# 256 units of a mixture layer kept per batch, not 512, with 256 more checked by signs

## The chip, the core and the metric

The kernel runs on one core of a Trainium2 chip. The metric is device time in microseconds of one execution on that core. Engines are named as the profile names them: PE (TensorE; PEld is its weight load), DVE (VectorE), ACT (ScalarE), POOL (GpSimd), SP (SyncE, which here only issues DMAs). A row "y<-vv,hh 128x256" reads: the instruction writes tile y from tiles vv and hh, 128 partitions by 256 elements.

## The reference

Attention through 49 agents feeds a mixture of eight experts, of which each token uses one. B, N, C = 4, 11456, 128; F = 1024 units per expert.

```python
agent_v = softmax(scale * agents @ k.T) @ v     # per batch: 49 x 128
x = softmax(scale * q @ agents.T) @ agent_v     # per token: 49 weights, then 128 values
e = argmax(x @ w_gate)
h = relu(x @ w1[e])                             # 1024 units
out = gate * sigmoid(x @ w_output_gate)[e] * (h @ w2[e])
```

A token enters only through its 49 weights, so `x @ w1[e]` is a product of those weights with the 49 x 1024 table `agent_v @ w1[e]`.

## The kernel before, in words

**Batches and units.** Each of the four batches has 12 units of tokens (eleven of 1024 and one of 192). For k a unit gives agent scores (tiles `ks`, `S`, `mx`), for v a weighted sum (`ev`, `av`), for q the token weights. When all k and v units of a batch are done, `folded` takes the agent averages, `choose` picks the expert that the batch's mean token would use, and its two weight matrices are loaded.

**Kept and linear units.** `hidden` (line 978) makes the 49 x 1024 table and a number g per unit, the smaller the more mixed the signs of its column. The 512 units with the smallest g are kept: `sel` gathers them, `ha` and `hr` make their first-layer weights `w` and `wr`, and `second` makes their second-layer weights `vv`. The others are taken to be of one sign for nearly all tokens, so that their relu is the identity or zero, and `linear` folds them into one matrix `G` (tile `gw`). A bound on g and on the token's squared weights (`thr`, `qe`) tells for which tokens this holds.

**A tile of 512 tokens** (92 tiles: 88 whole, four of 192). Single precision is carried as two half-precision parts. `q_rest` (line 1182) turns a unit's scores into weights `ef` and parts `e`; a transposing DMA puts them into `x_ld` (49 high rows, 49 low rows, 30 high rows again). `mm1` (line 1363) multiplies by `w` into four banks `h` and adds the 19 rows that did not fit by `wr`; for this three further DMAs copy rows of `x_ld` to other row groups (`x2`). `relu` takes `hh` (high part, ACT) and `hl` (rest, DVE) of each bank. `mm2` (line 1396) multiplies `gw`, and then `hh` and `hl` of each of four groups by `vv`, into `y`. `finish` adds the two halves of `y` (ACT `ys`, DVE `os`), `store` scales on POOL and writes out. Per unit `q_rest` also makes the eight expert logits (`lg`), the gate, and a flag per token.

**Left-over tokens.** Flagged tokens, and tokens of another expert, are gathered after the last unit of batches 0 and 1 (phase 0), and of 2 and 3 (phase 1): 14 tiles and 4 tiles of 128, exactly, in single precision (`let`, `lx`, `lh`, `ly`), with the expert's weights loaded anew for each. A loop behind them runs only when more tiles are needed.

**What sets the order.** The program is written by generators that a planner (`Clock`, `tick`) steps by estimated times; the result is one fixed list of instructions for each engine. Each engine runs its list in order. `spawn(g, prio)` gives the generator's rank, `LEFT` that of the left-over tiles, `ITEMS` (line 1338) the order in which k, v and q units are loaded and multiplied. On PE score products are written as blocks of 32 weight columns; when PE's list has a gap, as blocks of 64.

Of the kernel before, what the change touches and what calls it, by code (L numbers as in the profile page):

```python
# [17 lines left out]
P = 128  # L18
# [3 lines left out]
NBM = 4  # L22
NS = NBM * P
NG_ = 64
MARK = 1024.0
# [6 lines left out]
YS = 2  # L32

LARGE, SMALL, KEEP = 7, 8, 3
# [8 lines left out]
G4 = 4  # L43
# [11 lines left out]
K_W = K_GAM + NG_  # L55
# [4 lines left out]
QUIET = 4500.0  # L60
# [215 lines left out]
def agent_attention_top1_moe(ctx, tc, qT, kT, v, aT, wg, wo, w1, w2, cst, sides, slots, out):  # L276
# [53 lines left out]
    def group_free():  # L330

        if not all(banks[k][0] for k in range(G4)):
            return None
        return max(when_free(banks[k]) for k in range(G4))
# [39 lines left out]
    gam = kc[:, K_GAM:K_GAM + NG_]  # L374
    iot = cp.tile([P, NS], F16, name="iot")
# [3 lines left out]
    for i in range(2):  # L379
        t = cp.tile([P, 2, C], F16, name=f"gw_{i}")  # L380
        POOL.memset(t[:, 1, :], 0.0)
        gw.append(t)
    idle_x = cp.tile([P, 256], F16, name="idle_x")
# [10 lines left out]
    for i in range(4):  # L394
        t = cp.tile([P, 8, P], F16, name=f"e16_{i}")
        e16s.append(t)
# [74 lines left out]
    busy = {"w12": False, "sel": False}  # L471
# [104 lines left out]
    def scored(item):  # L576
        places[held.pop(item)][0] = True

# [112 lines left out]
    def v_weights(b, u, M):  # L691
# [8 lines left out]
        else:  # L700
            e = wk.tile([P, 4, C], F32, name=f"ev{b}_{u}", tag="os", bufs=4).rearrange("p t c -> p (t c)")
# [45 lines left out]
    def v_turned(u):  # L747
# [3 lines left out]
        if u in (0, FIRST):  # L751
            while not any(banks[k][0] for k in range(G4, 8)):
                yield None
            k = min((when_free(banks[k]), k) for k in range(G4, 8) if banks[k][0])[1]
# [10 lines left out]
        if u == NU - 4:  # L765
            others[:] = range(G4, 8)
# [18 lines left out]
    def shares():  # L785
# [9 lines left out]
        rec = wk.tile([P, A2], F32, name="rec0", tag="rec0")  # L795
# [104 lines left out]
    def choose(b, x, ad):  # L900
# [26 lines left out]
        while busy["w12"]:  # L927
            yield None
# [21 lines left out]
    def gates(b, ad):  # L950

        ab = wk.tile([P, A], F32, name=f"ab{b}", tag="ab")
# [25 lines left out]
    def hidden(b, ad, w1t, w2t):  # L978
# [34 lines left out]
        gv, gs = tl("hgv", C, F32, "avn")[:, 0:NG_], tl("hgs", 1)  # L1013
        yield from DVE.q.scalar_tensor_tensor(gv, c[:, 0:NG_], NS + 0.5, gam, op0=ALU.is_le, op1=ALU.mult)
        release(mark)
        yield from DVE.q.tensor_reduce(gs, gv, axis=AX.X, op=ALU.max)
        m, inc = tl("hm", NB), tl("hinc", NB)
# [6 lines left out]
        yield from DVE.q.scalar_tensor_tensor(inc, m, MARK, inc, op0=ALU.mult, op1=ALU.add)  # L1024
        yield from DVE.q.tensor_tensor(inc, c[:, 0:1].broadcast_to([P, NB]), inc, op=ALU.add)
# [3 lines left out]
        sel = wk.tile([P, NB, NS], F16, name=f"sel{b}", tag="sel16", bufs=1)  # L1029
        for n in range(NB):  # L1030
            yield from DVE.q.tensor_scalar(sel[:, n, :], iot, inc[:, n:n + 1], None, op0=ALU.is_equal)
# [955 lines left out]
```

## Time and profile before

| | |
|---|---|
| median of 3 runs (range) | 865.51 us (864.14 to 873.72) |
| profiled execution | 866.38 us, span 864.6 us |
| mean granted PE clock | 0.956 |
| busy PE, DVE, ACT, POOL | 735.0, 640.3, 445.8, 410.5 us |
| main tiles run | from 74.8 us to about 767 us |
| share of the 16 DMA engines by the main queue | 60.2% |

Busy time of PE counts each matmul from its issue to its modelled end, and matmuls overlap; how many fit into a stretch is read from the distance of their starts. Busy time of DVE, ACT and POOL is the time in which at least one instruction runs. An engine's idle time matters only where another waits for it.

### The profile page before, as it was taken

The page shows a single profiled execution, that of the slowest core. Times are in us where ns is not written, and L with a number is a line of the kernel's source. Part 1 is how long each engine was busy: PE and PEld are TensorE (multiplying, and loading weights), DVE is VectorE, ACT ScalarE, POOL GpSimd, SP SyncE. Part 2 cuts the span into 40 slices and gives each one's busy share as a digit, 9 for nine tenths or more (in the row PEclk, how much of TensorE's full clock was granted, in tenths as well). Part 3 has the DMA queues.
Part 4 walks back from the last instruction along what each step waited for, and adds up shares of the span by engine and source line. Part 5 has one row for each costly group of instructions (what it writes and reads, how often), then busy time and mean ns, then how long its engine had stood idle before and what let it go on. Part 6 is the DMA issues. An engine that isn't in the chain of part 4 may idle for free. (4 is left out here: it accounts for less than half of the span.)

```text
span 864.6 us, 31825 instructions
## 1 busy us (share of the span) xinstructions
PE 735.0 (85%) x12969; PEld 581.2 (67%) x12969; DVE 640.3 (74%) x2029; ACT 445.8 (52%) x1129; POOL 410.5 (47%) x794
## 2 busy tenths in 40 slices
PE   9989977889878998898998988877899999948644
PEld 8777755666666676666776666665687777847634
DVE  2945858878887888999897899878887999542210
ACT  2433645656645665657565655563575675413112
POOL 1001515766442587743443777543567465533131
PEclk9999989999999999999999999999999999969668
DMA  9993674866866777783587886754555343545312
GB/s 330 346 267 88 180 191 139 207 197 192 233 172 150 226 189 194 194 252 110 128 230 230 204 213 176 188 153 115 170 153 150 107 140 128 164 134 169 141 24 103
DMA packets 110039, 152.93 MB, mean 177 GB/s; under 512 B 62878, under 2 KB 71230, under 8 KB 109888
## 3 DMA queue, kind: packets, MB, share of 16 engines
q1 hardware_dynamic: 108160, 148.79, 60.2%
q0 software_dynamic: 1728, 2.06, 1.0%
q8 instruction: 103, 1.69, 0.8%
q14 instruction: 48, 0.39, 0.2%
HBM read 95.27 MB, written 35.43 MB: 151 GB/s over the span
## 5 line engine op out<-in xcount | busy, mean ns | idle before, releaser
L226 PE MATMUL y<-vv,hh 128*128 128x256 f16 (+1 forms) x1440 | 283.7, 274 | 0.1
L226 PE MATMUL y<-vv,hl 128*128 128x128 f16 (+1 forms) x1440 | 261.6, 219 | 1.2 <-issue 1.2
L226 DVE SCALAR_TENSOR_TENSOR hl<-h,hh 128x512 f16<-128x512 f32 (+1 forms) x368 | 226.0, 667 | 41.3 <-ACT hh L226 40.8
L226 ACT ACTIVATE hh<-h 128x512 f16<-128x512 f32 (+1 forms) x368 | 186.8, 591 | 74.9 <-PE h L226 74.5
L226 PEld LDWEIGHTS <-hh 128*128 128x128 f16 (+1 forms) x1440 | 142.2, 99 | 20.4 <-issue 2.2
L226 PEld LDWEIGHTS <-hl 128*128 128x128 f16 (+1 forms) x1440 | 143.4, 100 | 5.0 <-issue 1.7
L226 PE MATMUL y<-gw,x_ld 128*128 128x256 f16 x360 | 76.2, 275 | 52.6 <-DVE os L226 31.5
L226 ACT COPY ys<-y 128x256 f32<-128x256 f32 x179 | 67.0, 376 | 96.5 <-PE y L226 88.7
L226 POOL TENSOR_TENSOR os<-os,smt 128x512 f32<-128x512 f32 (+1 forms) x91 | 95.7, 1052 | 39.3 <-DVE os L226 31.9
L226 PEld LDWEIGHTS <-x_ld 128*128 128x128 f16 (+1 forms) x720 | 55.6, 100 | 75.8 <-issue 62.2
L226 PE MATMUL h<-x_ld,w 128*128 128x512 f16 (+1 forms) x368 | 104.9, 377 | 1.2 <-DVE hl L226 1.2
L226 DVE TENSOR_TENSOR os<-y,ys 128x256 f32<-128x256 f32 x179 | 73.7, 414 | 32.5 <-ACT ys L226 31.6
L226 POOL TENSOR_TENSOR e<-ef,e 128x392 f16<-128x392 f32 (+1 forms) x48 | 42.5, 886 | 33.9 <-ACT e L226 33.7
L226 PE MATMUL ks<-at,k_ld 128*32 128x50 f32 (+1 forms) x2120 | 51.4, 220 | 7.4 <-issue 7.0
L226 PEld LDWEIGHTS ks<-at,k_ld 128*32 128x32 f32 (+1 forms) x2120 | 44.2, 124 | 17.0 <-issue 12.1
L226 POOL TENSOR_TENSOR ev<-S,km_o 128x400 f32<-128x400 f32 (+1 forms) x36 | 33.0, 915 | 39.2 <-PE av L226 35.8
L226 PE MATMUL qs<-at,q_ld 128*32 128x50 f32 (+1 forms) x2768 | 44.8, 213 | 2.3 <-issue 1.3
L226 PEld LDWEIGHTS <-w 128*128 128x128 f16 x368 | 34.1, 101 | 18.1 <-issue 2.4
L226 PEld LDWEIGHTS qs<-at,q_ld 128*32 128x32 f32 (+1 forms) x2768 | 37.6, 113 | 11.6 <-issue 6.4
L226 ACT COPY S<-ks 128x400 f32<-128x400 f32 (+1 forms) x48 | 23.0, 480 | 39.0 <-PE ks L226 38.9
L226 PE MATMUL h<-x_ld,wr 19*128 19x512 f16 (+1 forms) x368 | 37.5, 384 | 3.1 <-DMA x_ld<-x_ld 3.1
L226 ACT ACTIVATE ef<-qz 128x392 f32<-128x392 f32 (+1 forms) x48 | 24.8, 516 | 26.5 <-DVE qz L226 22.6
(316 smaller groups left out, 1440.7 us busy)
## 6 DMA issues: line engine op xcount, KB each, us to landing
v_ld<-v SPq DMA_DIRECT2D x44, 512.0 KB, 4.6
q_ld<-qT SPq DMA_DIRECT2D x44, 512.0 KB, 4.0
out<-os SPq DMA_DIRECT2D x88, 256.0 KB, 4.5
k_ld<-kT SPq DMA_DIRECT2D x43, 512.0 KB, 4.5
lws<-w SPq DMA_DIRECT2D x18, 512.0 KB, 4.4
lw<-w SPq DMA_DIRECT2D x18, 512.0 KB, 4.1
efd<-ef SPq DMA_DIRECT2D x44, 200.0 KB, 4.4
x_ld<-x_ld SPq DMA_DIRECT2D x132, 64.0 KB, 3.5
```

The source lines that it names most:

```text
L226: return getattr(self.eng, op)(*a, **k)
```

## The change

256 units are kept per batch (`NBM` 2), so a tile has two groups, and `wr` is a 128-row tile with zeros below row 32, used without copies of `x_ld`. The next 256 units by g are linear as well, but each token is tested for them: `second_bound` finds them in two steps of 64 thresholds, and makes `wc`, the 49 x 256 table with each column's sign turned to that of its sum and its entries lowered by a small margin; `signs` multiplies each 128 tokens' high parts by `wc` (tile `ck`) and sums relu of the negated products on ACT (`cx`, `vs`). A token with a sum above zero is flagged. Beyond these 512 units the old bound holds. The logits are summed in PSUM, and some small steps of `q_rest` go from POOL to DVE or back. k and v units of all later batches follow the q units at a fixed rate of 2.2, where they came batch by batch; left-over tiles get rank 2, and their weights are loaded ahead into tiles of their own.

```diff
-NBM = 4
+NBM = 2
 NS = NBM * P
+NC_ = 256
+HB = 3
...
+OSN = 4
+FRONT, BACK = 6, 4
+
+LARGE, SMALL, KEEP = 7, 6, 3
...
-QUIET = 4500.0
+QUIET = 0.0
...
+    half_used = set()
+
+    def used(item):
+
+        if item in half_used:
+            scored(item)
+        else:
+            half_used.add(item)
...
-        yield "PE", [ax, sel], [o], 1
-        clk.vt["PE"] += TURN
         for n in range(NB):
-            for k in range(G4):
-                PE.matmul(o[32 * k:32 * k + 32, 0:P], ax[:, n, P:P + 32], sel[:, n, k * P:(k + 1) * P],
-                          start=(n == 0), stop=(n == NB - 1))
-        clk.vt["PE"] += TURN
-        rest = wk.tile([P, P], F16, name=f"wr{b}", tag="w0")
-        yield from DVE.q.tensor_copy(rest, o[:, 0:P])
+            yield from PE.q.matmul(o[0:32, 0:NS], ax[:, n, P:P + 32], sel[:, n, 0:NS], start=(n == 0), stop=(n == NB - 1))
+        rest = wrs[b % 2]
+        yield from DVE.q.tensor_copy(rest[0:32], o[0:32, 0:NS])
...
+        spawn(second_bound(b, g, m, gs, gc, gv, gs2, n1, m2, inc2, s_, tsv, sel), -1)
+        yield from linear(b, w2t, lin, tsv)
+    def second_bound(b, g, m, gs, gc, gv, gs2, n1, m2, inc2, s_, tsv, sel):
...
+        for step in range(2):
+            cmp_ = tl("hcm2", NB * NG_, F16).rearrange("p (n k) -> p n k", k=NG_)
+            yield from DVE.q.tensor_tensor(cmp_, gf.unsqueeze(2).broadcast_to(bc), gam2.unsqueeze(1).broadcast_to(bc),
+                                           op=ALU.is_lt)
...
+            for n in range(NB):
+                yield from PE.q.matmul(c[:, 0:NG_], idle_w, cmp_[:, n, :], start=(n == 0), stop=(n == NB - 1))
+            yield from DVE.q.scalar_tensor_tensor(gv, c[:, 0:NG_], n1, gam2, op0=ALU.is_le, op1=ALU.mult)
+            release(mark)
+            yield from DVE.q.tensor_reduce(dl if step else gs2, gv, axis=AX.X, op=ALU.max)
+            if step == 0:
+                yield from DVE.q.tensor_scalar(gf, g, gs2, float(NG_), op0=ALU.subtract, op1=ALU.mult)
+        yield from DVE.q.scalar_tensor_tensor(m2, gf, dl, m, op0=ALU.is_lt, op1=ALU.subtract)
...
+        for n in range(NB):
+            yield from DVE.q.tensor_scalar(sel[:, n, NS:NS + NC_], iot, inc2[:, n:n + 1], None, op0=ALU.is_equal)
...
+        o = bank(f"hd{b}")
+        mark = hold()
+        for n in range(NB):
+            yield from PE.q.matmul(o[0:A, 0:NC_], ac[:, n * A:(n + 1) * A], sel[:, n, NS:NS + NC_], start=(n == 0),
+                                   stop=(n == NB - 1))
+        wc = wcs[b % 2]
+        yield from ACT.q.copy(wc, o[0:A, 0:NC_])
+        release(mark)
+        st["wc"] = wc
...
-        while me > 3 and rests[me - 4] < 3 or me > 1 and not state.get(0, {}).get("w"):
+        while me >= FRONT and rests[me - FRONT] < 3 or me > 1 and not state.get(0, {}).get("w"):
...
-        while vacant_turned() is None:
-            yield None
-        x2 = place(("x2", b, u), vacant_turned()[1], [1024], F16)
-        for g in range(1, G4):
-            yield from SY.q.dma_start(x2[32 * g:32 * g + 32, 0:nt * pp], x1[0:32, 0:nt * pp])
-        X1[b, u] = x1, x2
+        X1[b, u] = x1
...
-            yield from PE.q.matmul(lg[0:pp, t * 36:(t + 1) * 36], x1[:, t * pp:(t + 1) * pp],
-                                   gs.rearrange("p k c -> p (k c)"), start=True, stop=True)
+            for k in range(2):
+                yield from PE.q.matmul(lg[0:pp, t * 18:t * 18 + 17], x1[:, t * pp:(t + 1) * pp], gs[:, k, 0:17],
+                                       start=(k == 0), stop=(k == 1))
...
+        L = lg[0:pp, 0:nt * 18].rearrange("p (t a) -> p t a", a=18)
+        lm, d, d256, rr = tl("lm"), tl("ld_", E), tl("d256"), tl("rr")
+        yield from DVE.q.tensor_reduce(lm, L[:, :, 0:E], axis=AX.X, op=ALU.max)
+        yield from DVE.q.tensor_tensor(d, L[:, :, 0:E], lm.unsqueeze(2).broadcast_to([pp, nt, E]), op=ALU.subtract)
+        yield from DVE.q.tensor_scalar(d256, L[:, :, 16], 1e-9, None, op0=ALU.add)
+        lo = tl("lo", E)
+        yield from ACT.q.copy(lo, L[:, :, E:2 * E])
+        vs = wk.tile([P, 8], F32, name=f"vs{b}_{u}", tag="vs", bufs=BACK)
+        spawn(signs(b, u, me, x1, vs), 1)
+        yield from POOL.q.tensor_scalar(rr, d256, s3[0:pp], None, op0=ALU.mult)
+        yield from DVE.q.reciprocal(rr, rr)
...
+        while me not in signed or "thr" not in state[b]:
+            yield None
         yield from DVE.q.scalar_tensor_tensor(d256, e2[0:pp, 0:nt], state[b]["thr"][0:pp], d256, op0=ALU.mult, op1=ALU.is_gt)
-        yield from POOL.q.tensor_tensor(og, d256.unsqueeze(2).broadcast_to([pp, nt, E]),
-                                        state[b]["dom"][0:pp].unsqueeze(1).broadcast_to([pp, nt, E]), op=ALU.mult)
-        yield from POOL.q.tensor_tensor(og, og, ndom[0:pp].unsqueeze(1).broadcast_to([pp, nt, E]), op=ALU.add)
+        yield from DVE.q.scalar_tensor_tensor(d256, vs[0:pp, 0:nt], 0.0, d256, op0=ALU.is_gt, op1=ALU.max)
+        yield from DVE.q.tensor_tensor(og, d256.unsqueeze(2).broadcast_to([pp, nt, E]),
+                                       ndom[0:pp].unsqueeze(1).broadcast_to([pp, nt, E]), op=ALU.max)
...
+    def signs(b, u, me, x1, vs):
+
+        base, pp, nt = UNITS[u]
+        while "wc" not in state[b] or me > 0 and me - 1 not in signed:
+            yield None
+        wc = state[b]["wc"]
+        for t in range(0, nt, 2):
+            yield from wait_free()
+            o = bank(f"ck{b}_{u}_{t}")
+            mark = hold()
+            for j in range(2):
+                yield from PE.q.matmul(o[0:pp, j * NC_:(j + 1) * NC_], x1[0:A, (t + j) * pp:(t + j + 1) * pp], wc,
+                                       start=True, stop=True)
+            for j in range(2):
+                x = wk.tile([P, NC_], F16, name=f"cx{b}_{u}_{t + j}", tag="cx", bufs=1)
+                yield from ACT.q.activation(x[0:pp], o[0:pp, j * NC_:(j + 1) * NC_], AF.Relu, scale=-1.0,
+                                            accum_out=vs[0:pp, t + j:t + j + 1])
+            release(mark)
+        used(("x1", b, u))
+        signed.add(me)
...
+        kv = [(kind, b, u) for b in range(1, B) for kind in "kv" for u in range(PRE if (kind, b) == ("k", 1) else 0, NU)]
+        qs = [("q", b, u) for b in range(B) for u in range(NU)][2:]
+        for i, x in enumerate(qs):
+            items.append(x)
+            n = max(0, int(RATE * (i + 1)) - int(RATE * i))
+            items += kv[:n]
+            del kv[:n]
...
+    RATE = 2.2
...
-    OFF = 8
-    RING = 12
+    OFF = 4
+    RING = 10
...
-        x1, x2 = (x[:, 512 * h:512 * h + w] for x in X1[b, u])
-        p = []
-        for g in range(G4):
-            p.append((bank(f"h{i}_{g}", k=g), hold()))
-            PE.matmul(p[g][0][:, 0:w], own_[:, g * P:(g + 1) * P], x1, start=True, stop=False)
-            if g < G4 - 1:
-                tick()
-        for g in range(G4):
-            rows = slice(32 * g, 32 * g + AR)
-            PE.matmul(p[g][0][:, 0:w], rest[rows, :], (x2 if g else x1)[rows, :], start=False, stop=True)
-        for g in range(G4):
-            spawn(relu(i, g, *p[g]), 0)
-        tick(0)
+        x1 = X1[b, u][:, 512 * h:512 * h + w]
+        for g in range(NBM):
+            o, mark = bank(f"h{i}_{g}", k=(NBM * i + g) % HB), hold()
+            PE.matmul(o[:, 0:w], own_[:, g * P:(g + 1) * P], x1, start=True, stop=False)
+            tick()
+            PE.matmul(o[:, 0:w], rest[:, g * P:(g + 1) * P], x1, start=False, stop=True)
+            spawn(relu(i, g, o, mark), 0)
+            tick()
...
-            if m1 < NT and G4 * (m1 + 1) - freed <= RING and group_free() is not None and group_free() <= now + 20.0:
+            if m1 < NT and NBM * (m1 + 1) - freed <= RING and group_free(m1) is not None and group_free(m1) <= now + 20.0:
...
-    LEFT = 5
-
-    ready, averaged = {}, {}
+    LEFT = 2
...
-                while (ph, k) not in ready or i > finished[0] + 1 or planning() or all(busy.values()):
+                while (ph, k) not in known or i > finished[0] + 1 or busy["own"] and (busy["sel"] or planning()):
                     yield None
-                home = "w12" if busy["sel"] else "sel"
+                home = "sel" if busy["own"] else "own"
                 busy[home] = True
-                t, ti, kk, _, ef, _, xt, two = ready[ph, k]
+                w1t, w2t = yield from left_load(ph, *known[ph, k], f"{ph}_{k}", home)
...
-        spawn(left_prepare(ph), 3 - 2 * ph)
+        spawn(left_prepare(ph), 1.5)
```

PE's list at a main tile. Before, in batch 3: the last of four products by `w`, four by `wr`, a block of q scores, then the first product of the second layer.

```order
L226 LDWEIGHTS w_13580
L226 MATMUL h_3_14055<-x_1_ld,w_13580 128x512
L226 LDWEIGHTS wr_13662
L226 MATMUL h_0_14036<-x_1_ld,wr_13662 128x512
L226 LDWEIGHTS wr_13662
L226 MATMUL h_1_14040<-x_1_ld,wr_13662 128x512
L226 LDWEIGHTS wr_13662
L226 MATMUL h_2_14047<-x_1_ld,wr_13662 128x512
L226 LDWEIGHTS wr_13662
L226 MATMUL h_3_14055<-x_1_ld,wr_13662 128x512
L226 MATMUL qs_5_14020<-at,q_5_ld 32x50 x32
```

Now, in batch 0:

```order
L231 LDWEIGHTS w_1302
L231 MATMUL h_0_4351<-x_10_ld,w_1302 128x512
L231 LDWEIGHTS wr_87
L231 MATMUL h_0_4351<-x_10_ld,wr_87 128x512
L231 LDWEIGHTS w_1302
L231 MATMUL h_1_4361<-x_10_ld,w_1302 128x512
L231 LDWEIGHTS wr_87
L231 MATMUL h_1_4361<-x_10_ld,wr_87 128x512
L231 MATMUL avn_4374<-kc,avd_104 49x128
```

Two banks are written instead of four, and each pair of products follows on its own bank. Over the whole list the products with `hh` and with `hl` fall from 1440 to 720 each, and 360 products `ck` of 256 columns are new.

ACT's list around two main tiles before, where the four `hh` stand together:

```order
L226 COPY ys_0_9860<-y_0_9833 128x256
L226 COPY ys_1_9889<-y_1_9857 128x256
L226 ACTIVATE ef_3_9874<-qz_3_9791 128x8x49
L226 ACTIVATE hh_0_9909<-h_0_9887 128x512
L226 ACTIVATE hh_1_9912<-h_1_9893 128x512
L226 ACTIVATE hh_2_9915<-h_2_9895 128x512
L226 ACTIVATE hh_3_9917<-h_3_9903 128x512
L226 ACTIVATE qz_3_9791<-ef_3_9874 128x8x49
```

Now, at the start of batch 2 (the `cx` belong to units of batch 1):

```order
L231 ACTIVATE hh_1_8116<-h_1_8109 128x192
L231 COPY ys_0_8166<-y_0_8118 128x256
L231 COPY lo_11_8174<-lg_11_8040 96x16
L231 ACTIVATE cx_8_2_8170,vs_8_7399<-ck_8_2_8162 128x256
L231 ACTIVATE cx_8_3_8182,vs_8_7399<-ck_8_2_8162 128x256
L231 ACTIVATE ef_0_8178<-qz_0_8134 128x8x49
L231 COPY ys_1_8204<-y_1_8163 128x256
L231 ACTIVATE cx_8_4_8207,vs_8_7399<-ck_8_4_8194 128x256
```

The 360 sums `cx` stand singly or in pairs between the copies `ys` and the steps of `q_rest`; the `hh` fall from 368 to 184.

PE's list behind the last product of the main tiles. Before (the first six of its rows; left-over tiles 8 to 13 of phase 0 and the table and 4 tiles of phase 1 follow):

```order
L226 MATMUL y_0_16931<-vv_13526,hl_3_16776 96x128
L226 MATMUL tbs_12_17004<-big_3_17000,ones 128x16
L226 MATMUL pbs_12_17022<-pptsb_0_9968,big_3_17000 128x128 x2
L226 MATMUL let_8_17032<-kc,big_2_16112 98x128
L226 MATMUL lx_8_17039<-let_sb_8_17034,lav_11411 128x128
L226 MATMUL lh_8_0_17057<-lxs_8_17046,lws_8_17009 128x128 x4
```

Now, where only phase 1 is left (its table, `pexc`, stands before the last tiles):

```order
L231 MATMUL y_0_15183<-vv_10630,hl_1_15061 96x128
L231 MATMUL tbs_0_15245<-big_0_15241,ones 128x32
L231 MATMUL pbs_0_15257<-pptsb_1_15125,big_0_15241 128x128 x4
L231 MATMUL let_0_15341<-kc,big_0_15241 98x128
L231 MATMUL lx_0_15345<-let_sb_0_15343,lav_15239 128x128
L231 MATMUL lh_0_0_15356<-lxs_0_15347,lw_0_15261 128x128 x4
```

Six left-over tiles and the table of phase 1 moved from behind the last main tile to between the main tiles.

## Rows read from the trace of the kernel before

**Rows 1.** Busy time of each engine in three stretches (before the first main tile, main tiles, behind the last): bounds and length in us, PE, PEld, DVE, ACT, POOL busy us (with instructions), granted PE clock, DMA share, GB/s.

```profile
0.00:75.00 75.00, 70.66 (x1058) 57.93 (x1059) 41.37 (x122) 24.93 (x60) 8.24 (x27) 0.98 0.81 274
75.00:767.00 692.00, 607.39 (x11543) 470.63 (x11541) 577.28 (x1800) 399.56 (x1016) 376.28 (x740) 0.98 0.64 175
767.00:865.00 98.00, 57.00 (x369) 52.62 (x369) 21.68 (x107) 21.26 (x53) 25.93 (x29) 0.74 0.35 118
```

**Rows 2.** The same view, shorter stretches.

```profile
350.00:400.00 50.00, 46.15 (x806) 35.61 (x805) 46.74 (x156) 34.76 (x93) 28.16 (x64) 1.00 0.73 200
...
275.00:400.00 125.00, 111.82 (x2362) 85.16 (x2360) 111.50 (x333) 80.28 (x205) 77.28 (x160) 1.00 0.74 202
...
610.00:767.00 157.00, 145.01 (x1826) 117.59 (x1822) 126.83 (x406) 91.47 (x235) 86.55 (x169) 0.99 0.47 139
...
825.00:850.00 25.00, 15.24 (x103) 13.97 (x104) 4.25 (x20) 5.85 (x15) 6.07 (x6) 0.72 0.28 94
```

**Rows 3.** Who waited for whom, on ACT and on DVE: us in total, times, longest.

```profile
ACT ys L226 <- PE y L226: 89.7, 84, 3.6
...
DVE hl L226 <- ACT hh L226: 40.8, 49, 3.2
```

**Rows 4.** PE's timeline in batch 1: start us, us of the merged run, instruction, count.

```profile
299.83 0.27 PE L226 MATMUL y<-gw,x_ld 128*128 128x256 f16 x1
299.94 0.27 PE L226 MATMUL y<-vv,hh 128*128 128x256 f16 x1
300.05 0.22 PE L226 MATMUL y<-vv,hl 128*128 128x128 f16 x1
300.11 0.27 PE L226 MATMUL y<-vv,hh 128*128 128x256 f16 x1
...
301.26 1.03 PE L226 MATMUL h<-x_ld,w 128*128 128x512 f16 x4
302.22 0.40 PE L226 MATMUL h<-x_ld,wr 19*128 19x512 f16 x4
302.55 0.92 PE L226 MATMUL qs<-at,q_ld 128*32 128x50 f32 x64
303.39 0.28 PE L226 MATMUL y<-gw,x_ld 128*128 128x256 f16 x1
...
305.12 0.18 PE L226 MATMUL lg<-gs,x_ld 128*128 128x36 f16 x1
305.15 0.27 PE L226 MATMUL y<-vv,hh 128*128 128x256 f16 x1
```

**Rows 5.** Groups of instructions by shape on ACT and DVE: count, busy us, mean ns of one, idle before.

```profile
L226 ACT ACTIVATE hh<-h 128x512 f16<-128x512 f32 x352 | 182.8, 602 | 70.0 <-PE h L226 69.5
L226 ACT COPY ys<-y 128x256 f32<-128x256 f32 x176 | 65.9, 376 | 94.4 <-PE y L226 87.4 <-DVE os L226 3.6 <-issue 1.3
...
L226 DVE SCALAR_TENSOR_TENSOR hl<-h,hh 128x512 f16<-128x512 f32 x352 | 221.2, 681 | 39.5 <-ACT hh L226 39.0
...
L226 DVE TENSOR_SCALAR rr<-d,s_s 128x8 f32<-128x8 f32 x44 | 13.8, 316 | 0.0
L226 DVE TENSOR_TENSOR oh<-lr,rm 128x64 f32<-128x64 f32 x44 | 13.6, 310 | 0.1
...
L226 DVE SCALAR_TENSOR_TENSOR a<-se,d 128x8 f32<-128x8 f32 x44 | 11.4, 260 | 0.3
L226 DVE TENSOR_SCALAR sel<-iot,hinc 128x512 f16<-128x512 f16 x32 | 9.5, 366 | 0.0
...
L226 DVE TENSOR_TENSOR hcmp<-hg,kc 128x512 f16<-128x512 f32 x4 | 2.8, 693 | 0.0
```

**Rows 6.** ACT's timeline: two activations with a sum, and a copy of 256 columns with what follows it.

```profile
53.15 0.64 ACT L226 ACTIVATE wsq<-w1t 128x512 f16<-128x512 f32 x1
53.68 0.20 ACT L226 ACTIVATION_READ_ACCUMULATOR wsq<-w1t 128x1 f32 x1
53.77 0.63 ACT L226 ACTIVATE wsq<-w1t 128x512 f16<-128x512 f32 x1
...
300.48 0.40 ACT L226 COPY ys<-y 128x256 f32<-128x256 f32 x1
300.73 0.57 ACT L226 ACTIVATE qz<-ef 128x392 f32<-128x392 f32 x1
```

**Rows 7.** Timelines of PE and DVE behind the last main tile: the table of phase 1 (`pexc`, `tbs`), its index, its first tile (`let`), and the products of its second and last tile.

```profile
788.36 0.29 PE L226 MATMUL pexc<-tot,kc 128*128 128x16 f32 x2
...
803.51 0.61 PE L226 MATMUL tbs<-big,ones 128*128 128x32 f32 x2 [6.23 <-DVE big L226]
...
813.53 0.17 DVE L226 CAST lrus<-lrgs 128x4 uint32<-128x4 f32 x1
826.41 0.53 DVE L226 TENSOR_TENSOR big<-big,lppxs 128x360 f32<-128x360 f32 x1 [12.71 <-DMA big<-cumd,lrus]
...
833.18 0.45 PE L226 MATMUL let<-kc,big 128*98 128x128 f32 x1 [14.80 <-DVE big L226]
...
840.98 1.95 PE L226 MATMUL lh<-lxs,lw 128*128 128x128 f32 x16
842.78 2.33 PE L226 MATMUL ly<-lw,lh 128*128 128x128 f32 x16
...
852.38 2.05 PE L226 MATMUL ly<-lw,lh 128*128 128x128 f32 x16
```

More of the change, by code (lines that the diff above doesn't have):

```diff
@@ L382, in agent_attention_top1_moe @@
         gw.append(t)
+    wrs = []
+    for i in range(2):
+        t = cp.tile([P, NS], F16, name=f"wr_{i}")
+        POOL.memset(t, 0.0)
+        wrs.append(t)
+    wcs = [cp.tile([A, NC_], F16, name=f"wc_{i}") for i in range(2)]
     idle_x = cp.tile([P, 256], F16, name="idle_x")
@@ L470, in agent_attention_top1_moe @@
     state = {}
-    busy = {"w12": False, "sel": False}
+    busy = {"own": False, "sel": False}
     picking = [True]
@@ L751, in v_turned @@
         if u in (0, FIRST):
[L752 removed]
+            while not any(banks[k][0] for k in range(HB, 8)):
                 yield None
[L754 removed]
+            k = min((when_free(banks[k]), k) for k in range(HB, 8) if banks[k][0])[1]
             k0["avp"] = bank(f"avT{u}", k=k), hold()
@@ L1038, in hidden @@
         for n in range(NB):
-            yield from PE.q.matmul(o, ax[:, n, 0:P], sel[:, n, :], start=(n == 0), stop=(n == NB - 1))
+            yield from PE.q.matmul(o[:, 0:NS], ax[:, n, 0:P], sel[:, n, 0:NS], start=(n == 0), stop=(n == NB - 1))
         w = wk.tile([P, NS], F16, name=f"w{b}", tag="w1")
-        yield from ACT.q.copy(w, o)
+        yield from ACT.q.copy(w, o[:, 0:NS])
         release(mark)
@@ L1190, in q_rest @@
         yield from DVE.q.tensor_reduce(m[0:pp, 0:nt], sv, axis=AX.X, op=ALU.max)
+        while me > 1 and me - 2 not in squared:
+            yield None
         z = wk.tile([P, 8, A2], F32, name=f"qz{b}_{u}", tag="qz", bufs=2)
@@ L1274, in q_rest @@
         yield from DVE.q.reciprocal(T, a_)
-        while not {"i12", "thr"} <= state[b].keys():
+        while "i12" not in state[b]:
             yield None
@@ L1427, in finish @@
         if k == 0:
-            while i > 3 and i - 4 not in done or i > 1 and i - 2 not in summed:
+            while i >= OSN and i - OSN not in done or i > 1 and i - 2 not in summed:
                 yield None
-            OS[i] = wk.tile([P, 4, C], F32, name=f"os{i}", tag="os", bufs=4)
+            OS[i] = wk.tile([P, 4, C], F32, name=f"os{i}", tag="os", bufs=OSN)
+        while i not in OS or k > halves.get(i, 0):
+            yield None
         os = OS[i]
@@ L1825, in planning @@
     def planning():
-        return any(K[b]["v"] >= NU - 3 and not (state.get(b, {}).get("vv") and "G" in state[b]) for b in K)
+        return any(K[b]["v"] >= NU - 3 and not (state.get(b, {}).get("vv") and {"G", "wc"} <= state[b].keys()) for b in K)
     def left_static():
```

187 lines of the change are left out of this document (103 added, 84 removed).

## The prediction

> **What bounds the kernel now.** The first view is the table of engine busy time by stretch [rows 1]. Nothing of the main tiles runs in the first 75 us, in which the keys and values of batch 0 are loaded and its weights prepared. Then come 692 us of main tiles, and 98 us of left-over tiles. In the main stretch DVE is busy for 577.3 us, 83.4%, PE for 607.4 us by modelled ends, ACT for 399.6, POOL for 376.3; the DMA engines work 64% of it. So two engines share the bound. Shorter stretches show it [rows 2]: DVE reaches 93.5% from 350 to 400 us, and 89.2% from 275 to 400; from 610 to 767, where no key or value work is left, PE is at 92% and DVE at 81%.
>
> The waits [rows 3] say the same from the other side: ACT's largest, 89.7 us, is for `y` of PE, and DVE's largest, 40.8 us, for `hh`, which itself follows PE. ACT has room, and what waits on it waits in turn for PE.
>
> How much PE can be relieved is read from the distance of starts on its timeline [rows 4], not from busy time. A 256-column product takes 0.11 us to the next start, a pair `hh`, `hl` 0.17 (299.94 to 300.11), four products by `w` 0.96 (0.24 each), four by `wr` together 0.33, a block of q scores 0.84, one `lg` 0.03.
>
> **The main tiles on PE.** Half a tile has two `gw` products and eight pairs: 0.22 + 8 x 0.17 = 1.58 us. With two halves, 0.96 + 0.33 for the first layer and four `lg`, a tile costs 3.16 + 1.29 + 0.12 = 4.57. After, there are four pairs per half, 2 x (0.22 + 0.68) = 1.80; two products by `w`, 0.48; two by the full-height `wr`; four `ck` of 256 columns, 0.44; eight narrower `lg`, at most 0.24. For `wr` the rows give two ends, 2 x 0.33 / 4 = 0.17 as now and 2 x 0.24 = 0.48 as for `w`; since it now has all 128 rows and follows `w` on its own bank, I take 0.48. The tile is 3.44 us, 1.13 less, and 88 whole tiles and four of three eighths make 89.5: **101 us off PE**. The Trainium skill, "TensorEngine Tiling (Array Packing)", section "When to Use Tiling", speaks against this edit: a contraction of 32 rows should use fourfold row tiling. The trace agrees, in that four `wr` of 19 rows take 0.33 us; by that rule alone a packed `wr` would save a further 0.31 us per tile, some 28 us of PE.
>
> **DVE.** It loses half the `hl`: 176 x 221.2 / 352 [rows 5] = 111 us. Per unit of `q_rest` it loses two small steps (`rr`, the sum of the logits) and gains four (the logits' difference, `ogs` by `rr`, the maximum with `vs`, the flag's spreading). Net two steps in 48 units, at 0.26 to 0.32 us as `a` and `rr` are: 28 us. `sel` is written in 64 half-width instructions, not 32: its 9.5 us stay or double, I take 5 more. `second_bound` has per batch two comparisons of 512 like `hcmp` (1.4), one of 392 (0.6), 14 small ones at about 0.28 (3.9): 24 us in four batches. Six left-over tiles and a table come in from behind the main tiles, with about half of the 21.7 us that DVE has there [rows 1]: 10 us. Main stretch: 577 - 111 + 28 + 5 + 24 + 10 = **533 us**.
>
> **ACT.** 184 `hh` go, 93 us (0.52 each in the group [rows 5]). 360 `cx` come. The lower end of one is from the timeline [rows 6]: a 256-column copy hands on after 0.25 us, and reading a sum adds 0.09 (53.68 to 53.77): 0.34. The upper end is the whole of both, 0.376 + 0.20 = 0.58. That is 122 to 207 us; in a queue that has other work behind each, the lower end is nearer, and I take 0.40, 144 us. Some 17 us come with the six left-over tiles and the second bound. Sum: 400 - 93 + 144 + 17 = 468 us, 531 at the upper end.
>
> **The rest.** POOL loses three 64- or 128-column steps per unit and gains one small one, and takes no wait with it. The three row copies per unit leave SP's queue and the DMA engines; the transposing DMA is now the last step ahead of `mm1`, but it also was before for the first group, and units are prepared some tiles ahead. The added wait of `q_rest` for `signs` delays the flags and the gathered rows, not `smt`, which `store` needs; up to four units may hang there. The even flow of k and v puts their blocks beside all q units; the last batches' averages are ready sooner (`ha` of batch 3 stands 228 of 360 `gw` products into PE's list, before at 268, its batch starts at 270), so a batch change should cost less; I count nothing for it. DMA work is 64% of the main stretch now and comes to about 72% of a 610 us one, with fewer bytes: covered; where a load is late, `scores` waits first. PE's list has more 64-wide blocks, which the planner writes only into its gaps.
>
> **Front and tail.** Before the first tile `ha` and four `sel` shrink by about 1 us: 74. Behind the last main tile PE's list now has only the index of phase 1 and 4 tiles. From `tbs` at 803.5 [rows 7] to the end of the span that is 61 us, in which DVE waited 12.7 us for gathers (issued behind scatters of phase 0 that will be done by then), 5 of which I take off; for the part of the table that may still be open I add 4. Tail: **60 us**, where it was 98. The six tiles cost PE in the main stretch 6 x (1.80 + 2.05 + 0.6 for `let` and `lx`) = 27 us.
>
> **The sum.** PE by starts: 89.5 tiles of 4.57 are 409 us, some 115 blocks 97, eight left-over tiles 36, and the products per batch about 35 by my estimate: 577. After: 577 - 101 + 27 + 3 = 506. So DVE with 533 is the fullest. In the old main stretch it ran at 83.4%, where it set the pace at 89.2%, at best at 93.5%. PE falls behind it, but ACT comes closer; I take 87%: 533 / 0.87 = 613. Total 74 + 613 + 60 = 747, and 1.8 us lie outside the span in the profiled execution of before (866.38); the median is 0.9 below that. **748 us, 13.6% less.**
>
> **Rivals.**
> 1. *Denser.* With PE relieved and batch changes smoothed, DVE runs at 93.5% throughout: 533 / 0.935 = 570, total 706. For it: DVE's waits [rows 3] go back to PE. Against: ACT. Chance 0.20.
> 2. *ACT's sums delay the relus.* `hh` stands in one queue behind `cx`, so the three `h` banks come free late, and DVE waits more than now. At the upper price ACT has 531 us, as much as DVE, and two full engines in a row run at 80% or worse: 533 / 0.80 to 533 / 0.74, total 804 to 858. Chance from 775 up 0.16.
> 3. *Slower than before: the sums end on the path.* If each `ck` holds a bank and each `cx` is waited for before the next `hh` can go, then the chain PE to ACT to PE sets the pace: 692 - 101 + 27 + 207 = 825, total 961. It decides from the point where the main stretch exceeds 738 us (874 in total), which is 120 of the 207 us, 0.33 us of every `cx`. For it: 4 `cx` per tile stand among 2 `hh` and 2 `ys`. Against: nothing of the next tile needs a `cx`, five banks are left besides the three. Chance 0.09.
> 4. *The clock falls.* Granted was 0.72 of full speed in the tail, with PE at 61% busy, and 1.00 where it was at 89% [rows 2]. With gaps in every tile, at 0.72 throughout, PE has 506 / 0.72 = 703 us and is the bound: total 839. The Trainium skill, "TensorE: Matmul & The Clock Gate", section "HAM oscillation — how this bites in real kernels", describes this: a loop in which PE runs dry in every round starts each round at the lower clock. By starts PE would be 506 / 613 = 83% full, as before (577 / 692 = 83%), so the trace gives it little: 0.04.
> 5. *More left-over tiles.* The new flags could take more than 14 and 4 tiles and start the loop at the end, at some 45 us per tile (index 30, one tile with its loads 15 [rows 7]). Worked out on the reference's inputs, flagged and foreign tokens go from 1346 to 1352 in phase 0 and from 368 to 371 in phase 1, still 14 and 4 tiles. Chance 0.02, total 793.
>
> **Numbers.** The forecast's own case, DVE at 83.4 to 89.2%, spans 733 to 775 and has 0.49. With rival 1 down to 695 (it may also be that DVE's load is 10 us less) and rival 2 up to 815, with rival 5, about 0.8 is held: 695 to 815. About 1% can be told from no change. Faster by more: 0.49 + 0.20 + 0.15 + 0.02 + part of rival 4, 0.87. Within 1%: 0.04. Slower: 0.09.
>
> **What would show it.** In the changed profile: 184 `hh` and `hl`; 360 `cx` with their reads, 0.34 to 0.58 us each; DVE busy near 570 us in all; ACT near 515; PE's `wr` 0.24 apart; only four `let` behind the last `y`, and some 60 us there. It is wrong if ACT's waits on PE stay at 90 us while PE waits for `hh`, if the granted clock drops below 0.9 in the middle, or if DVE falls below 80%.

## The result and the profile after

The changed kernel took **804.3 us** (median of four executions, 795.7 to 809.0), the kernel before 866.8 beside it; their ratio is 0.920 (95% interval 0.909 to 0.930). That ratio rests on the two shorter of the four, so the better reference is the first experiment below, the same kernel again: **807.8 us** (six executions, 806.7 to 811.5), ratio 0.934 (0.930 to 0.938). The kernel is faster, and within the range given; but the gain is 58 to 63 us, where 118 were forecast. The execution profiled is the shortest, 795.7 us with a span of 794.0.

First the busy time by stretch, with the columns of [rows 1]: before the first main tile, main tiles, behind the last.

```profile
0.00:68.00 68.00, 65.01 (x1007) 54.27 (x1008) 41.76 (x121) 24.92 (x62) 9.24 (x30) 0.97 0.86 296
68.00:734.00 666.00, 593.69 (x9169) 435.04 (x9168) 537.46 (x1863) 462.62 (x1592) 361.38 (x668) 0.94 0.63 178
734.00:794.00 60.00, 22.99 (x154) 21.15 (x151) 13.63 (x55) 9.63 (x24) 14.47 (x15) 0.68 0.27 86
```

Read length against length: the front went from 75 to 68 us, the tail from 98 to 60, and the main stretch, where half of the kept units was taken away, only from 692 to 666. So 45 of the 71 us saved in the profiled executions came from the two ends. With one measure for both kernels it is more: 734 is the end of the last `y`, but the 767 of [rows 1] lies 6 us behind it, since the last `y` before is

```profile
761.00 0.22 PE L226 MATMUL y<-vv,hl 128*96 128x128 f16 x1
```

By the last `y` the main stretch went from 686 to 666 us and the tail from 103 to 60. In the middle the loads are those forecast, to within 1.2%: DVE 537 us (533 forecast), ACT 463 (468). What is not as forecast is how full they are: DVE 537 / 666 = 80.7%, not 87%. PE is at 594 / 666 = 89% by modelled ends, no less than before (607 / 692 = 88%): it was not relieved as the forecast had it. The granted clock fell too: 0.94 on average, where it was 0.98. Between the levels 2.4 and 1.2 GHz that is 2 x 0.06 x 666 = 80 us at the lower one, before 2 x 0.02 x 692 = 28.

Next, who waited for whom (us in total, times, longest), to be read against [rows 3] and against a row of the kernel before that they leave out:

```profile
ACT hh L226 <- PE h L226: 74.5, 81, 3.8
```

```profile
ACT ys L231 <- PE y L231: 35.2, 53, 2.4
ACT cx L231 <- PE ck L231: 34.5, 50, 3.1
...
ACT hh L231 <- PE h L231: 29.3, 35, 2.5
...
DVE hl L231 <- ACT hh L231: 15.0, 30, 1.7
...
PE y L231 <- ACT cx L231: 11.5, 17, 2.3
```

ACT still waits for PE, now in three parts, 99 us in all; before, `y` and `h` alone made 164 (89.7 and 74.5). PE waits for `cx` too, but for little.

PE's timeline shows what the new products cost it (start, us of the merged run, instruction, count):

```profile
138.37 0.27 PE L231 MATMUL y<-vv,hh 128*128 128x256 f16 x1
138.57 0.39 PE L231 MATMUL ck<-wc,x_ld 49*128 49x256 f16 x2
138.90 0.23 PE L231 MATMUL y<-vv,hl 128*128 128x128 f16 x1
...
302.66 0.27 PE L231 MATMUL y<-vv,hh 128*128 128x256 f16 x1
302.77 0.22 PE L231 MATMUL y<-vv,hl 128*128 128x128 f16 x1
302.82 0.27 PE L231 MATMUL y<-vv,hh 128*128 128x256 f16 x1
...
487.87 0.38 PE L231 MATMUL h<-x_ld,w 128*128 128x512 f16 x1
488.09 0.38 PE L231 MATMUL h<-x_ld,wr 128*128 128x512 f16 x1
488.30 0.38 PE L231 MATMUL h<-x_ld,w 128*128 128x512 f16 x1
488.52 0.38 PE L231 MATMUL h<-x_ld,wr 128*128 128x512 f16 x1
```

An `hh` of 256 columns still goes on after 0.11 us, and `w` and the full-height `wr` after 0.22 (0.24 was taken). Two `ck`, also of 256 columns each, take 0.33 us to the next start (0.32 in the median): **0.16 each, not 0.11**. Their stationary operand has 49 rows. And the price does not stop at the `ck`: the `hh` in front of them goes on after 0.20 us, not 0.11. From that `hh` to the `hl` behind are 0.53 us, where three products at 0.11 take 0.33.

ACT's timeline has the price of a `cx` and of the reading of its sum:

```profile
301.03 0.40 ACT L231 ACTIVATE cx<-ck 128x256 f16<-128x256 f32 x1
301.31 0.21 ACT L231 ACTIVATION_READ_ACCUMULATOR cx<-ck 128x1 f32 x1
301.40 0.54 ACT L231 ACTIVATE ef<-qz 128x392 f32<-128x392 f32 x1
```

From `cx` to what follows are 0.37 us, where 0.40 was taken (and 0.34 to 0.58 bounded).

### The profile page after: what moved, and what is told of

Its sections match the earlier page's. It is cut to its first block, busy times and chain, and to the rows that moved or that the text cites. A ratio compares the mean times of both kernels' runs of the same rounds, so it can differ in the third digit from the quotient of the medians.

```text
span 794.0 us, 26954 instructions
## 1 busy us (share of the span) xinstructions
PE 681.7 (86%) x10325; PEld 510.5 (64%) x10325; DVE 592.8 (75%) x2037; ACT 497.2 (63%) x1677; POOL 385.1 (49%) x712
## 5 line engine op out<-in xcount | busy, mean ns | idle before, releaser
L231 PEld LDWEIGHTS <-x_ld 128*128 128x128 f16 (+3 forms) x1440 | 107.2, 100 | 98.5 <-issue 61.6
L231 PE MATMUL y<-vv,hh 128*128 128x256 f16 x720 | 164.8, 279 | 0.0
L231 ACT ACTIVATE cx<-ck 128x256 f16<-128x256 f32 x360 | 140.0, 389 | 38.4 <-PE ck L231 34.5
L231 PE MATMUL y<-vv,hl 128*128 128x128 f16 x720 | 144.5, 224 | 0.0
L231 DVE SCALAR_TENSOR_TENSOR hl<-h,hh 128x512 f16<-128x512 f32 (+1 forms) x184 | 119.0, 668 | 16.6 <-ACT hh L231 15.0
L231 ACT ACTIVATE hh<-h 128x512 f16<-128x512 f32 (+1 forms) x184 | 103.0, 590 | 31.9 <-PE h L231 29.3
L231 PE MATMUL ck<-wc,x_ld 49*128 49x256 f16 x360 | 77.9, 289 | 9.4 <-ACT cx L231 3.9
L231 PEld LDWEIGHTS <-hh 128*128 128x128 f16 x720 | 72.6, 101 | 13.5 <-issue 5.1
L231 ACT ACTIVATION_READ_ACCUMULATOR cx<-ck 128x1 f32 x360 | 73.9, 205 | 0.0
L231 PE MATMUL h<-x_ld,wr 128*128 128x512 f16 (+1 forms) x184 | 72.3, 394 | 0.0
```

Source lines behind the costliest of these rows:

```text
L231: return getattr(self.eng, op)(*a, **k)
```

## The experiments

Three theories for the 53 us that the main stretch is longer than forecast (666, not 613). **Theory 1**: ACT's sums hold up the relus and PE's next products. **Theory 2**: TensorE's time is still the bound, and `ck` takes more of it than counted. **Theory 3**: neither; DVE and the written order set the time. In the four edits that take something away or change a shape (the next four sections), the planner counts as it did, so that every remaining instruction keeps its place.

### The same kernel again, and the test left out

> The changed kernel once more, on the chip of the three runs beside it, so that each of them has its own reference: 795 to 810 us, ratio to the kernel before 0.91 to 0.93, by every theory. The last `y` at 725 to 745 us, the `ck` 0.16 us from the start of one to the start of the next, 70 to 85 us of the stretch between the first `h` and the last `y` at half the clock.

Measured: 807.8 us, in the range expected; the profiled execution has the last `y` at 748.3, and 2 x 0.09 x 681 = 123 us of the main stretch at the lower clock, both more than expected. It is 13 us longer than the execution shown above with the same instructions, and has 43 us more at the lower clock: that is what executions of this kernel differ by. Its main stretch is 15 us longer for the 43, about a third of a us for each.

```profile
67.00:748.00 681.00, 607.46 (x9171) 441.18 (x9169) 538.91 (x1861) 464.65 (x1592) 361.21 (x668) 0.91 0.61 174
```

Without products and sums (`ghost` counts an instruction in the plan and doesn't issue it):

```diff
-                yield from PE.q.matmul(o[0:pp, ...], x1[0:A, ...], wc, ...)
+                yield from ghost(PE, "matmul", o[0:pp, ...], x1[0:A, ...], wc, ...)
...
-                yield from ACT.q.activation(x[0:pp], ..., accum_out=vs[0:pp, t + j:t + j + 1])
+                yield from ghost(ACT, "activation", x[0:pp], ..., accum_out=vs[0:pp, t + j:t + j + 1])
```

> Leaves out the test of the next 256 units for each token: neither the 360 products `ck` nor the 360 `cx` that read them are made, and the sums `vs` are zero, which changes the order of nothing else on any engine. It measures what the test costs in all. Theory 1 (ACT's sums hold the relus and PE's next products up): 60 to 80 us less, since the sums go with the products. Theory 2 (TensorE's time is the bound, and each `ck` takes 0.16 us of it): 360 x 0.16 = 58 us less, and some 5 to 10 of waits on `cx`, so 735 to 745 us. Theory 3 (neither: the fullest engine is DVE, and the rest is the order written for it): less than 25 us, 780 us or more.

Measured: **752.9 us**, ratio 0.870 (0.866 to 0.874), 55 us less than the kernel beside it. That is about the gap to the forecast, and it lies between the ranges of theories 2 and 3. Its main stretch:

```profile
68.00:691.00 623.00, 518.33 (x8805) 418.32 (x8804) 538.00 (x1860) 328.79 (x872) 364.05 (x715) 0.93 0.66 190
```

DVE has the same 538 us and is now at 86.4%, nearly the 87% of the forecast, although the clock is hardly better.

### Products made, but not read

Only the second half of that edit.

> Leaves out the reading of the products only: the 360 `ck` are made as in the changed kernel, the 360 `cx` on ACT and their sums are not, `vs` is zero; all other instructions keep their order. Against the run without products it has PE's part alone, against the changed kernel it lacks ACT's part alone. Theory 1 (ACT's sums are what costs): nearly all of the gain of the run without products comes here already, 740 to 755 us. Theory 2 (TensorE's time): only the waits on `cx` go, 11.5 + 3.9 us of PE's idle time and a few of ACT's own, so 780 to 795 us. Theory 3: 795 us or more.

Measured: **791.8 us**, ratio 0.912 (0.907 to 0.917): 16 us less than with the reading. So of the 55 us, taken off in this order, 16 are ACT's part and 39 PE's. Theory 1 is left with the smaller share. The waits show why:

```profile
ACT ys L231 <- PE y L231: 86.6, 102, 3.6
ACT hh L231 <- PE h L231: 58.2, 68, 3.6
```

ACT, freed of 360 `cx`, hands little of the time on: it waits 145 us for PE's `y` and `h`, where with the sums it waited 74 for them (39.4 and 34.1) and 39 for `ck`. So most of what ACT gains it waits for PE.

### The same products with all rows

```diff
-    wcs = [cp.tile([A, NC_], F16, name=f"wc_{i}") for i in range(2)]
+    wcs = []
+    for i in range(2):
+        t = cp.tile([P, NC_], F16, name=f"wc_{i}")
+        POOL.eng.memset(t, 0.0)
+        wcs.append(t)
...
-        yield from ACT.q.copy(wc, o[0:A, 0:NC_])
+        yield from ACT.q.copy(wc[0:A], o[0:A, 0:NC_])
...
-                yield from PE.q.matmul(o[0:pp, ...], x1[0:A, ...], wc, ...)
+                yield from PE.q.matmul(o[0:pp, ...], x1[:, ...], wc, ...)
```

> Computes the same: `wc` has 128 rows, of which rows 49 to 127 hold zeros, and the stationary operand of `ck` is all 128 rows of `x1` in place of the first 49; no instruction moves. If a stationary operand of 49 rows is what makes a `ck` take 0.16 us (its load stands beside no product), it takes 0.11 here, 360 x 0.05 = 18 us of PE less: by theory 2 (TensorE's time is the bound) 783 to 792 us, by theory 1 (ACT's sums) and theory 3 (DVE) 798 us or more. If the rows don't matter, 0.16 stays and so does the time.

Measured: **777.9 us**, ratio 0.900 (0.897 to 0.904): 30 us less, for 79 rows of zeros more per product, and below every range given. The same place on PE's timeline, and the main stretch:

```profile
134.38 0.27 PE L231 MATMUL y<-vv,hh 128*128 128x256 f16 x1
134.49 0.38 PE L231 MATMUL ck<-wc,x_ld 128*128 128x256 f16 x2
134.71 0.22 PE L231 MATMUL y<-vv,hl 128*128 128x128 f16 x1
```

```profile
67.00:715.00 648.00, 554.89 (x9171) 444.37 (x9170) 537.52 (x1862) 459.43 (x1592) 362.48 (x668) 0.96 0.65 183
```

Two `ck` now take 0.22 us, 0.11 each, which is worth the 18 us expected. The `hh` ahead of them goes on after 0.11 us again, and that had not been counted: from `hh` to `hl` are 0.33 us, where it was 0.53. Such places, one or more `ck` with a product on either side, number 199 in both lists; in the 115 that ran at full clock and without a wait in both, the difference is 0.20 us in the median. Added up from the trace's starts, all 199 take 135 us in the same kernel with 49 rows and 109 here. So 26 of the 33 us by which the main stretch is shorter (681 and 648) are gone from these places themselves, and the price is that of **changing from operands of 128 rows to 49 and back**, about 0.1 us each way; from one `ck` to the next with 49 rows are 0.12. The kernel before paid it too: the four `w` of [rows 4] take 0.96 us because three go on after 0.22 and the last, ahead of a `wr` of 19 rows, after 0.31 (medians of 57 such groups).

The clock rose as well, from 0.91 to 0.96: 2 x 0.04 x 648 = 52 us at the lower level, not 123. In all six executions of this kernel the mean clock of the whole span was 0.931 to 0.945, in the six of the other 0.902 to 0.912, so it isn't chance. But the products of 49 rows are not what lowers it: the run without any `ck` has 0.93 in its main stretch as well. Why it is highest with full-height `ck`, and how much of the 30 us it is worth, was not settled. The Trainium skill, "TensorE: Matmul & The Clock Gate", section "LDWEIGHTS (loading the stationary operand)", says that a load's time hangs on the operand's columns and not on its rows. The trace agrees on the load's own duration (102 and 96 ns below); when a load starts, which is what differs here, is another matter. These are the loads with 128 and with 49 rows in the kernel with both (busy us, mean ns of one, idle time before):

```profile
L231 PEld LDWEIGHTS <-x_ld 128*128 128x128 f16 x1056 | 81.5, 102 | 50.2 <-issue 27.2 <-DVE os L231 3.3 <-DMA x_ld<-e 0.7
...
L231 PEld LDWEIGHTS <-x_ld 49*128 49x128 f16 x352 | 24.3, 96 | 51.8 <-issue 37.6 <-DVE d L231 1.8 <-DVE os L231 1.7
```

The idle time before one load is 0.15 us with 49 rows (51.8 / 352) and 0.05 with 128 (50.2 / 1056): the load is no longer, it starts later. Why was not looked into.

### Narrow blocks throughout

The planner writes blocks of scores in pieces of 32 columns beside the tiles, and of 64 in its idle moments; to the next start a 64-wide block takes 1.07 us of PE (median of 43 in the version with all rows), a 32-wide one 0.84 [rows 4]. This run, and all that follow, stand on the version with all rows; here each 64-wide piece behind the front is issued as two of 32 in its place.

```diff
-                PE.matmul(dst, x[:, h:h + c], m, start=(not last or i == 0), ...)
+                for g in range(0, c, PART):
+                    d = min(PART, c - g)
+                    PE.eng.matmul(dst[g:g + d], x[:, h + g:h + g + d], m, **k)
```

> The version with `ck` over all 128 rows, and in it every block of the scores and of the products with the values is written in pieces of 32 columns, also those that the planner's idle moments now write in pieces of 64; the order of all instructions is the same. Theory A (the wide pieces are what leaves TensorE 85 us of excess over its usual starts: a 64-wide block of 16 takes 1.07 us at full clock, and two of 32 columns that do the same work 0.84): 243 pieces of 64 per group of records, some 150 blocks, so 20 to 35 us less, 745 to 758 us. Theory B (they are waits or half clock that only fall into these blocks): 773 to 783 us. Theory C (the narrow ones take the longer, since each loads a stationary operand of its own): 785 us or more.

Measured: **790.5 us**, ratio 0.911 (0.906 to 0.916), 12 slower, though every block by itself is shorter. PE's waits and a piece of its timeline (`issue` is time in which the engine waited for nothing that the profile shows):

```profile
PE av L543 <- issue: 12.8, 6, 2.9
PE qs L543 <- issue: 12.2, 12, 3.2
...
PE ks L543 <- issue: 9.1, 3, 3.7
```

```profile
289.78 0.82 PE L543 MATMUL av<-ev,v_ld 128*32 128x50 f32 x52
292.75 0.37 PE L543 MATMUL av<-ev,v_ld 128*32 128x50 f32 x12 [2.15 <-issue]
```

The block is cut in two by 2.15 us in which no data is missing. All such waits at blocks are 34 us here; in the version with wide pieces they are 2.6, nearly all of it in this row:

```profile
PE ks L231 <- issue: 2.4, 2, 1.7
```

PE has 1844 products and as many weight loads more in its list. That it runs out of instructions at the dense places fits these rows, but no row shows it. The clock of the main stretch is lower too, 0.94 and not 0.96. Theory A falls; theory C has the sign, and the instruction that it names (a load for each piece) is half of what was added.

### The old order of keys and values

```diff
-        kv = [(kind, b, u) for b in range(1, B) for kind in "kv" ...]
...
+        for b in range(B):
+            qs = [("q", b, u) for u in range(2, NU)]
...
+                for i, (nk, nv) in enumerate(MIX if b > 0 else MIX0):
```

> The version with `ck` over all 128 rows, with the order of keys and values of the kernel before (lists MIX0 and MIX) in place of 2.2 of them after each query unit. The prediction put nothing on the new order. If the order is worth nothing, 773 to 783 us; if it is what fills the places where the batch changes, and the loss of the middle comes from elsewhere, slower, 785 to 800; if the new order, which leaves the last third without keys and values, is what loses the missing time, 750 to 770 with less of half clock after 480 us.

Measured: **789.3 us**, ratio 0.913 (0.908 to 0.917), 11 slower. Its main stretch is 651 us, like the 648 of the version with the new order; what is longer is the tail, 68 us, with six left-over tiles behind the last `y`, where that version has four. By itself this doesn't decide on the order, since the runs below move as much.

### Orders that the planner writes otherwise

Three runs let the planner count a running sum on ACT longer (110, 60 and 160 ns); one lets its own tally of PE's columns see the 128 rows of `ck`; the last does this and 110.

```diff
         if self.name == "ACT":
-            return (51.0 if ins[0].name in self.clk.psum else 93.0) + ...
+            return (110.0 if k.get("accum_out") is not None else 0.0) + (51.0 if ...
```

> The version with `ck` over all 128 rows, and the planner counts 110 ns more for an ACT instruction with a running sum (it counts 264 ns for a `cx`, and the trace has 0.34 to 0.40 us from one to the next), so it puts them further apart and writes another order. Leaving the 360 out altogether while the products stayed gave 16 us, and that is the most that a better place can give. If the waits of PE and of the relus on ACT's `cx` (13.4 + 6.6 us of PE's idle time in the version it starts from) come from the planner's wrong count: 762 to 772 us. If they come from ACT's load: 774 us or more.

Measured: **762.0 us**, ratio 0.879 (0.874 to 0.885), 16 us less than with the count unchanged: it looked like the planner's wrong price.

> As the run in which the planner counts 110 ns more for a running sum on ACT, with 60 ns more. Any change of a planned cost writes another order from its first difference on, so the 16 us of that run may be its count or the luck of its order. If the count is what matters, this lies between the two: 764 to 775 us, with ACT's waits on `ck` and PE's on `cx` between theirs. If the order's luck is: anywhere from 762 to 790 us, with no relation to the count.

> The same with 160 ns more (424 ns for a `cx`, above the 0.34 to 0.40 us that the trace has). If the count is what matters, 757 to 767 us, no worse than with 110, since a `cx` planned too long costs only a little idle time of ACT, which is at 65 to 75% of the middle. If it is the order's luck: anywhere from 762 to 790 us.

Measured: 773.3 us, ratio 0.893 (0.890 to 0.897), with 60; 782.6, ratio 0.906 (0.902 to 0.910), with 160. With 60 there is a gain of 5 us, between the two as the count would have it; but 160, which should have been as good as 110, is the slowest of all.

> `ck` over all 128 rows, with no cost of the planner changed on purpose: only its own tally of TensorE's recent columns now counts `ck` with 128 rows instead of 49, and the clearing of the two `wc` tiles stands in its plan, which is enough to write another order from the start. It computes the same and tells how far the time moves by the order alone: 774 to 782 us if orders are alike (the reason for the count then stands), 762 to 792 us if they are not.

Measured: 766.7 us, ratio 0.886 (0.883 to 0.890), with no price changed at all. (Only the tally differs from the version of 777.9 us; the clearing of `wc` stands outside the plan here too.) The wait that the theory named is in no relation to the time either. PE's `y` waited for `cx` 13.4 us in the version of 777.9 us, 8.2 in that of 762.0, 11.4 in that of 782.6, and here:

```profile
PE y L231 <- ACT cx L231: 12.0, 28, 1.7
```

> `ck` over all 128 rows, the planner's tally of TensorE's columns counts it so, and a running sum on ACT is planned 110 ns longer: the two kernels that were shortest so far (762.0 and 766.7 us), in one. If what each changed in the plan were worth something by itself, 750 to 760 us; if each was only another order, this is one more draw: 762 to 785 us.

Measured: 765.1 us, ratio 0.886 (0.882 to 0.890): one more draw. So the theory of the planned sums falls. Six lists of one computation, all with `ck` over 128 rows, took 762.0, 765.1, 766.7, 773.3, 777.9 and 782.6 us (0.879 to 0.906 of the kernel before, timed beside each); **the order alone moves this kernel by up to 20 us**. What makes a good list good was not found; their main stretches, 629 to 653 us, carry the difference. The shortest beats both kernels, 0.879 of the one before and 46 us under the changed one.

### Unused products to hold the clock

```diff
-        if mains[0] == 0 and clk.columns(t) < (...) and k is not None:
+        if clk.columns(t) < (...) and k is not None:
```

> The version with `ck` over all 128 rows, and the planner may put unused 256-column products on TensorE also after the middle has begun, wherever it has nothing else to write and counts little work behind it: 13 of them between the first `h` and the last `y`, and 136 behind. Nothing of the result depends on them. If the clock of the tail costs what its rows say (719.5 to 750.2 us at half the clock, with `let`, `lx` and the first `lh` in it): the tail gets 3 to 8 us shorter, 770 to 775 us, and the middle stays within 5 us. If the tail is DVE's and the DMAs' alone: 776 to 781 us.

Measured: 780.8 us, ratio 0.900 (0.896 to 0.904): no change in all, but two that cancel.

```profile
68.00:699.00 631.00, 550.50 (x9170) 434.37 (x9168) 525.29 (x1821) 451.27 (x1573) 357.34 (x659) 0.96 0.63 182
699.00:784.00 85.00, 59.77 (x413) 52.46 (x411) 19.35 (x97) 17.53 (x44) 21.07 (x24) 0.82 0.35 107
```

The trace has more unused products than were expected in the middle, 52 between the first `h` and the last `y`, and 114 behind. The middle is 17 us shorter, at the same clock of 0.96; that is within what an order is worth, and no run tells the two apart. The tail is 26 us longer, though its clock rose from 0.68 to 0.82, because seven left-over tiles stand behind the last `y` and not four; two of the three more:

```profile
714.82 0.45 PE L231 MATMUL let<-kc,big 128*98 128x128 f32 x1 [3.58 <-DVE big L231]
...
722.84 0.27 PE L231 MATMUL let<-kc,big 128*98 128x128 f32 x1
```

A better clock in the tail was worth nothing that can be seen beside that. The tail is a matter of how many tiles are left when the middle ends.

## Why the prediction was right and wrong

**Right: the tail.** 60 us forecast, 60 measured, and between 56 and 61 in every list with four or five `let` behind the last `y`. As in [rows 7], it is the table of phase 1 and the wait of its first tile; from `tbs` to the first `let` are 24 us, 30 before, and 5 less were forecast:

```profile
737.96 0.38 PE L231 MATMUL tbs<-big,ones 128*128 128x32 f32 x2 [3.70 <-DVE big L231]
761.72 0.42 PE L231 MATMUL let<-kc,big 128*98 128x128 f32 x1 [19.34 <-DVE big L231]
```

Behind the main tiles 38 us less are spent, 43 by the last `y`, the largest part of the difference. It is not all gain: the six tiles now take time of PE in the main stretch, 27 us by the forecast's own count, and no run puts them back. Which of the edits (the streams' ranks, the weights loaded ahead) moves them was not tried either.

**Right: the loads.** 184 `hh` and `hl`, DVE at 593 us in all (570 forecast: the front's 41.8 and the tail's 13.6 were higher than counted), ACT 497 (515), a `cx` at 0.37 us, `wr` at 0.22 where 0.24 was taken. The front was 6 us shorter than taken.

**Wrong: "PE falls behind it, but ACT comes closer; I take 87%: 613."** It failed twice over. The term of the sum that was mis-sized is `ck` at 0.11 us: with its neighbours it costs 26 us more, since I had read its price from products with 128 rows in [rows 4] and gave no range for 49, although for `wr` I had bounded such a price from both sides. The sign of it stood in those rows: I read the 0.96 us of four `w` as 0.24 each, where it is the change to `wr` that makes the last one longer. And PE was counted at full clock: for the 52 us more at the lower level the two executions of the same kernel (15 us for 43) give some 18, an estimate. Together that is 44 of the 53 us, if the two add, which no run shows: with all rows, and 52 us at the lower clock, the main stretch is still 648. What the runs do show is that the step from DVE's load to the length was wrong: DVE's 538 us stayed, and the main stretch followed PE, 681 to 648 us for the rows of zeros (with what the clock gave), and 664 to 623 without the products; ACT's sums made 17 (681 to 664). So DVE did not set the pace, and the pace that the forecast took for it is reached only by the run without the test, 86.4% in a main stretch of 623 us.

**Rival 2 (ACT's sums delay the relus)** gave 804 to 858 and holds the measured time, but by a mechanism that has only 16 us; its figures of 80 and 74% came from no row. The range given went up to 815 for this rival's sake, so that the measured time lies inside it is in part luck. **Rival 4 (the clock falls)** had been given 0.04, with the clock at 0.72 throughout; what came was smaller, 0.94 and 0.91 in the two executions. The sign I named for it, below 0.9 in the middle, appears in parts alone, such as the second of these (window, length, then as above):

```profile
400.00:500.00 100.00, 81.68 (x1321) 57.58 (x1321) 87.52 (x288) 69.55 (x231) 54.80 (x91) 0.91 0.74 208
500.00:600.00 100.00, 87.97 (x980) 63.10 (x980) 76.23 (x291) 64.39 (x233) 58.23 (x110) 0.88 0.55 153
```

There lie the last change of batch (`hc` from 489.9 us, `ha` at 501.7, `hd` from 536.7) and the first left-over tiles (`let` from 521.8). **Rivals 1, 3 and 5** did not occur: DVE was at 80.7% and not 93.5, the sums cost 16 us and not 207, and the left-over tiles were 14 and 4.

**Right by luck: "PE's list has more 64-wide blocks"**, which I costed at nothing. They take more PE time by starts, and are still the better choice, by 12 us in the one list in which both were tried.

## What to carry to other kernels

Price a new product together with the products on either side of it, from rows with the same number of stationary rows, and where there are none, bound it from both sides; padding with zeros to the height of its neighbours made it shorter here and is worth a try. When work is taken from a bound engine, look at what the same change gives it back, and at the clock, before the next engine is made the bound. And before a gain of 2% is put down to an edit in a kernel whose order is written by a planner, time two or three other orders of the same instructions.

## What was not expected of the hardware

- Two products with 49 stationary rows between products with 128 cost 0.20 us more than the same two padded to 128: half of it on the product ahead of them (0.20 us to the next start, not 0.11), half on the second of the two.
- The same edit raised the mean clock of the main stretch from 0.91 to 0.96 without any instruction moved; with no such products at all it was 0.93.
- PE stopped for up to 3.7 us inside dense blocks of small products with nothing to wait for in the profile; two narrow products for each wide one raised these waits from 2.6 us to 34.
